# Transposing attention keys inside their load buffers, with one ring of five buffers for every large load

## The chip, the cores and the metric

The kernel runs on one NeuronCore of one Trainium2 chip. The metric is the device time of one execution in microseconds; lower is better. The engines are named as in the profile: PE is TensorE (PEld its weight loads), DVE is VectorE, ACT is ScalarE, POOL is GpSimd and SP is SyncE, whose queue issues nearly all DMAs here.

## The reference

A decode step for two sequences: attention over the last 4096 keys of a cache, beside a dense layer with the mish activation. Both read the same normalised input, and both results are added to it. All data are bfloat16.

```
x: [2, 1, 448]   k_cache, v_cache: [2, 8, 32768, 256]   wq: [448, 4096]   wo: [4096, 448]
w1: [448, 1792]  b1: [1792]   w2: [1792, 448]

xn = (x - mean) / sqrt(var + 1e-5)
q  = xn @ wq                                  # 16 query heads of 256
k, v = the last 4096 positions of the caches  # 8 heads, each for 2 query heads
A  = softmax(q . k / 16) @ v, heads joined, @ wo
h  = xn @ w1 + b1
B  = (h * tanh(softplus(h))) @ w2
out = x + A + B
```

## The kernel before

**Tiles and stages.** The four units `u` = 0 to 3 each hold two key heads of both sequences. The keys of a unit come as two loads k(u,0) and k(u,1), the values as two loads v(u,0) and v(u,1), each 4096 KB: 32 KB in each of 128 partitions. Beside them there are `wq` (3584 KB), `w1` (1568 KB), `w2` (1568 KB in four pieces), a piece `wo(u)` of 896 KB for each unit, and the small `b1` and `x`. SP issues all of them but `x`.

**Buffers.** `ring(name)` takes the next of three 32 KB buffers of `kv_pool`; keys, values, `wq`, `w1` and `w2` all go through it. A load into a buffer waits until what was in it three loads earlier has been read. Two more 32 KB buffers, `kt0` and `kt1` in `kt_pool`, hold transposed keys. `wo` has a pool of its own with two buffers.

**Steps for a unit.** `turns(u, i)` (L266) lets DVE transpose the 32x32 blocks of k(u,i), seen as 4-byte words, in two instructions of 128x4096 from the load buffer into `kt[i]`. After that the load buffer is free. `scores(u, i)` (L340 on) starts a PSUM bank with a mask matmul (L345), adds 32 matmuls over `kt[i]` (L356), lets ACT take the exp (L364), and for i = 1 lets DVE bring the weights into the layout that the values need (L367, and `swap`, L336 to L338). `weigh(u)` adds up the weights (L380, L388). `values(u, g)` (L402) multiplies v(u,g) by the weights, 32 matmuls for a load. `gather(u)`, `finish(u)`, `relay(u)` and `mix_early(u)` (L414 to L482) divide, lay out and multiply by `wo(u)`.

**Beginning.** After constants and the normalisation, PE makes the queries from `wq` (`project`, L291 to L324). `dense_in` (L510, L519) multiplies by `w1` and adds `b1`, and `mish` (L533 to L544) applies the activation. They stand after `turns(0, 1)` in the program.

**End.** The last unit's v(3,1) comes in three pieces (40, 16 and 8 of 64 rows per partition) and `w2` in four, so that PE can begin on each as it lands; `values_fixed` (L435) takes the last two pieces of the values, and `mix` and `dense_out` add into `acc` (L249). `pace(n)` (L575) issues n matmuls whose results nobody reads.

**Order.** The schedule is manual: each engine runs its instructions in the order in which the program writes them, and each load is issued by SP in that order, waiting for its buffer first. The order of loads is wq (two halves), k(0,0), k(0,1), b1, w1, and then for each unit k(u+1,0), v(u,0), k(u+1,1), v(u,1), wo(u), until the last unit's values, wo(3) and `w2`.

Of the kernel before, what the change touches and what calls it, by code (L numbers as in the profile page):

```python
# [11 lines left out]
BF16 = mybir.dt.bfloat16  # L12
FP32 = mybir.dt.float32
# [4 lines left out]
def kernel(  # L18
# [13 lines left out]
    nc = tc.nc  # L32
    P = 128
    G = 4
    J = 4
    R = 4
    RK = 2
# [10 lines left out]
    U = Hkv // KU  # L48
    C = P // J
    CT = W // C  # L50
    T = CT // R
# [16 lines left out]

    lead_pool = ctx.enter_context(tc.tile_pool(name="lead", bufs=1))
    lead_pool.tile([P, 192], BF16, name="lead")  # L70
    kv_pool = ctx.enter_context(tc.tile_pool(name="kv", bufs=3))
    kt_pool = ctx.enter_context(tc.tile_pool(name="kt", bufs=1))
    wo_pool = ctx.enter_context(tc.tile_pool(name="wo", bufs=2))
    p_pool = ctx.enter_context(tc.tile_pool(name="pp", bufs=1))
    consts = ctx.enter_context(tc.tile_pool(name="consts", bufs=1))
# [13 lines left out]
    def ring(name):  # L89
        return kv_pool.tile([P, RK * KE], BF16, tag="kv", name=name)  # L90
# [3 lines left out]
    def load_k(u, r):  # L94
        t = ring("k")
        src = kview[u][:, s0:, :].rearrange("j (c t) d -> c j (t d)", c=C)
        nc.sync.dma_start(out=t[:], in_=src[:, :, r * RK * KE : (r + 1) * RK * KE])
        k_t[u, r] = t
# [19 lines left out]
    nc.scalar.dma_start(out=x_bf[:, :], in_=A_x.flatten_outer_dims())  # L118
    b1_sb = consts.tile([2, F2], BF16)

    wq = ring("wq")
    wq_in = A_wq.flatten().rearrange("(p e) -> p e", p=P)
    half = NS * HW // 2
    for lo in (0, half):
        nc.sync.dma_start(out=wq[:, lo : lo + half], in_=wq_in[:, lo : lo + half])
    wq_t = [wq[:, i * HW : (i + 1) * HW] for i in range(NS)]
    load_k(0, 0)
    load_k(0, 1)
    nc.sync.dma_start(out=b1_sb[:], in_=B_b1.rearrange("(k f) -> k f", k=2))

    ident = consts.tile([P, P], BF16)
    make_identity(nc, ident[:])
# [114 lines left out]
    def add_rows(lhsT, rows, stop=False):  # L247
# [7 lines left out]
                skip_group_check=True,  # L255
            )

    kt = [
        kt_pool.tile([P, T * NB, RK, P // (R * J), J], FP32, name=f"kt{i}") for i in range(NH)
    ]  # L260
    ktm = [
        kt[i][:].bitcast(BF16).rearrange("p (t n) r c (j e) -> p n e t (r c j)", n=NB, e=2)
        for i in range(NH)
    ]

    def turns(u, i):  # L266
        t = k_t.pop((u, i))
        for r in range(RK):
            nc.vector.transpose(  # L269
                out=kt[i][:, :, r, :, :],  # L270
                in_=t[:, r * KE : (r + 1) * KE].bitcast(FP32).rearrange(
                    "p (a c j) -> p a c j", c=P // (R * J), j=J
                ),
            )

    spread = {}
    for n in range(2):
# [9 lines left out]
    def project():  # L287
        q_ps = ps_m.tile([P, 512], FP32, tag="m", name="q_ps")
        for s in range(NS):
            for u in range(U):  # L290
                nc.tensor.matmul(  # L291
                    q_ps[32 * u : 32 * (u + 1), :],
                    lhsT=xs[:, s, :],
                    rhs=wq_t[s][:, u * 512 : (u + 1) * 512],
                    start=(s == 0),
                    stop=(s == NS - 1),
                    skip_group_check=True,
                )
        q_sb = small.tile([P, 4, P], BF16, tag="vs", name="q_sb", bufs=1)
        nc.scalar.copy(out=q_sb[:].rearrange("p a m -> p (a m)"), in_=q_ps[:])  # L300
        qt_ps = ps_m.tile([P, 4, P], BF16, tag="m", name="qt_ps")
        for a in range(4):
            nc.tensor.transpose(qt_ps[:, a, :], q_sb[:, a, :], ident[:])  # L303
        qT = consts.tile([P, 2, U, Bsz, KU, rep], BF16)
        q_v = qt_ps[:].rearrange("p (h c) (u r) -> p c u r h", c=2, u=U)
        for c in range(2):
            for b in range(Bsz):
                nc.vector.tensor_copy(  # L308
                    out=qT[:, c, :, b, :, :], in_=q_v[:, c, :, b : KU * Bsz : Bsz, :]
                )  # L310
        qr_ps = ps_m.tile([P, 2 * NB, U, NQ], FP32, tag="m", name="qr_ps")
        for n in range(NB):
            for e in range(2):
                nc.tensor.matmul(
                    qr_ps[:, 2 * n + e, :, :].rearrange("p u q -> p (u q)"),
                    lhsT=spread[n % 2, e][:].rearrange("p g a -> p (g a)"),
                    rhs=qT[:, n // 2].rearrange("p u b k h -> p (u b k h)"),
                    start=True,
                    stop=True,
                    skip_group_check=True,  # L320
                )
        for g in range(G):
            rows = slice(g * 32, (g + 1) * 32)
            nc.vector.tensor_copy(  # L324
                out=qd[rows, :, :, g, :],
                in_=qr_ps[rows].rearrange("p n u q -> p u n q"),
            )
# [12 lines left out]
    def scores(u, i):  # L340
        if i == 0:
            state["ex"] = small.tile([P, T, 4, NH, J], BF16, tag="ex", name="ex", bufs=1)
        ex = state["ex"]
        sc = ps_sc.tile([P, T, 4, J], FP32, tag="sc", name="sc")
        nc.tensor.matmul(  # L345
            sc[:].rearrange("p t c m -> p (t c m)"),
            lhsT=ident[:],
            rhs=mneg[:].rearrange("p a j -> p (a j)"),
            start=True,
            stop=False,  # L350
            skip_group_check=True,
        )
        for n in range(NB):
            for e in range(2):
                for w in range(4):
                    nc.tensor.matmul(  # L356
                        sc[32 * w : 32 * (w + 1)].rearrange("p t c m -> p t (c m)"),
                        lhsT=qd[:, u, 2 * n + e, :, :].rearrange("p g q -> p (g q)"),
                        rhs=ktm[i][:, n, e, :, 16 * w : 16 * (w + 1)],
                        start=False,  # L360
                        stop=(n == NB - 1 and e == 1),
                        skip_group_check=True,
                    )
        nc.scalar.activation(out=ex[:, :, :, i, :], in_=sc[:], func=ACT.Exp, scale=scale)  # L364
        if i == NH - 1:
            for h in range(NH):
                nc.vector.transpose(  # L367
                    out=p_all[:, :, h * TH : (h + 1) * TH, :].rearrange("p g t q -> p t g q"),
                    in_=ex[:, h * TH : (h + 1) * TH].rearrange(
                        "p t c i m -> p t (c i m)"  # L370
                    ).rearrange("p t (g q) -> p t g q", g=G),
                )
            swap()
# [121 lines left out]

    act_bf = consts.tile([P, NI, 2, Bsz], BF16)

    def load_w1():
        t = ring("w1")
        nc.sync.dma_start(  # L500
            out=t[:, 0 : NS * F2], in_=B_w1.flatten().rearrange("(p e) -> p e", p=P)
        )
        state["w1"] = t

    def dense_in():
        w1 = state.pop("w1")
        w1_v = w1[:, 0 : NS * F2].rearrange("p (s q i) -> p s i q", s=NS, i=NI)
        h_ps = ps_m.tile([P, NI, 2, Bsz], FP32, tag="m", name="h_ps")
        for i in range(NI):
            nc.tensor.matmul(  # L510
                h_ps[:, i, :, :].rearrange("p k b -> p (k b)"),
                lhsT=b1_sb[:, i::NI],
                rhs=halves[:].rearrange("p k b -> p (k b)"),
                start=True,
                stop=False,
                skip_group_check=True,
            )
            for s in range(NS):
                nc.tensor.matmul(  # L519
                    h_ps[:, i, :, :].rearrange("p k b -> p (k b)"),  # L520
                    lhsT=w1_v[:, s, i, :],
                    rhs=xs[:, s, 0 : 2 * Bsz],
                    start=False,
                    stop=(s == NS - 1),
                    skip_group_check=True,
                )
        state["h"] = h_ps
# [37 lines left out]
                act_bf[:, i, k, :], state["w2"][:, at : at + D], stop=(k == 1 and i == NI - 1)  # L565
            )

    load_w1()
    def pace(n, key=None):
        ps = ps_sc.tile([P, T, 4, J], FP32, tag="sc", name="pace")  # L570
        for i in range(n):
# [9 lines left out]
                skip_group_check=True,  # L581
            )

    project()
    turns(0, 0)
    scores(0, 0)
    turns(0, 1)
    dense_in()
    mish()
    scores(0, 1)  # L590
    weigh(0)
    for u in range(U - 1):
        load_k(u + 1, 0)
        load_v(u, 0)
        load_k(u + 1, 1)
        load_v(u, 1)
        load_wo(u)
        turns(u + 1, 0)
        values(u, 0)
        scores(u + 1, 0)  # L600
        turns(u + 1, 1)
        if u == U - 2:
            pace(11, key=ktm[1][:, 0, 0, :, 0:16])
        values(u, 1)
        gather(u)
        finish(u)
        scores(u + 1, 1)
        relay(u)
        mix_early(u)
        if u < U - 2:  # L610
            weigh(u + 1)
    u = U - 1
    load_v(u, 0)
    load_v(u, 1, 0, 40)
    load_wo(u)
    load_v(u, 1, 40, 56)
    load_v(u, 1, 56, TV)
    for part in range(len(w2_parts)):
        load_w2(part)
    pace(3)  # L620
    carry()
    pace(5)
# [57 lines left out]
```

## Time and profile before

| What | Value |
|---|---|
| Median of 3 runs | 188.95 us (188.94 to 189.04) |
| Profiled execution, span from first to last instruction | 187.3 us |
| Time around the span (median less span) | 1.65 us |
| DMA bytes | 77.67 MB from HBM, mean 415 GB/s over the span |
| Busy: PE, DVE, ACT | 84.5 us, 92.8 us, 12.4 us |
| Transposes of the keys (L269) | 16, 70.0 us together, 4414 ns each |

The execution's own total is not printed on the page; the time around its span is therefore taken against the median of the runs. In the profile's groups, "x16 | 70.0, 4414 | 33.8 <-DMA k" means 16 instructions, 70.0 us busy together, 4414 ns each on average, and 33.8 us in which the engine stood idle just before them, most of it until a load of k had landed. In a table by stretches, each engine has its busy time and its count of instructions, and the last three columns are the clock granted to TensorE, the mean busy share of the 16 DMA engines, and GB/s.

### The profile page before, as it was taken

The page shows a single profiled execution, that of the slowest core. Times are in us where ns is not written, and L with a number is a line of the kernel's source. Part 1 is how long each engine was busy: PE and PEld are TensorE (multiplying, and loading weights), DVE is VectorE, ACT ScalarE, POOL GpSimd, SP SyncE. Part 2 cuts the span into 40 slices and gives each one's busy share as a digit, 9 for nine tenths or more (in the row PEclk, how much of TensorE's full clock was granted, in tenths as well). Part 3 has the DMA queues.
Part 4 walks back from the last instruction along what each step waited for, and adds up shares of the span by engine and source line. Part 5 has one row for each costly group of instructions (what it writes and reads, how often), then busy time and mean ns, then how long its engine had stood idle before and what let it go on. Part 6 is the DMA issues. An engine that isn't in the chain of part 4 may idle for free.

```text
span 187.3 us, 1938 instructions
## 1 busy us (share of the span) xinstructions
PE 84.5 (45%) x847; PEld 37.4 (20%) x847; DVE 92.8 (50%) x93; ACT 12.4 (7%) x26; POOL 4.7 (2%) x16
## 2 busy tenths in 40 slices
PE   0373015893119000882047002881065068789694
PEld 0211002551003000340012000430021023424353
DVE  6704397974792097038940296048920593040100
ACT  3003000101000100110001000110001000210100
POOL 8100000000000000000000000000000000000000
PEclk9999999955557955599558855698559756999999
DMA  6999999999999999999999999999999999999991
GB/s 215 422 483 427 441 406 408 454 444 448 427 434 413 416 436 406 462 448 441 441 434 402 413 441 422 445 444 434 448 427 420 420 427 434 434 422 408 416 403 45
DMA packets 4195, 77.78 MB, mean 415 GB/s; under 512 B 470, under 2 KB 732, under 8 KB 1628
## 3 DMA queue, kind: packets, MB, share of 16 engines
q1 hardware_dynamic: 4184, 77.67, 97.1%
q8 instruction: 6, 0.10, 0.2%
q14 instruction: 1, 0.01, 0.0%
q10 hardware_dynamic: 4, 0.00, 0.0%
HBM read 77.67 MB, written 0.00 MB: 415 GB/s over the span
## 4 chain that ended last, share of the span: by engine, by line
DMA 64%; DVE 15%; PE 15%; issue 3%; ACT 1%; SPq 1%
DMA v<-in_A_v_cache_dram 32%; DMA k<-in_A_k_cache_dram 15%; DVE kt L269 12%; DMA w<-in_B_w_dram 11%; DMA wq<-in_A_wq_dram 6%; PE pv L402 4%; PE sc L356 3%; PE h_ps L519 2%; DVE p L367 1%; PE acc L249 1%; PE q_ps L291 1%; PE dn L380 1%; DVE rec L388 1%; PE o L435 1%; ACT ex L364 1%
## 5 line engine op out<-in xcount | busy, mean ns | idle before, releaser
L269 DVE STREAM_TRANSPOSE kt<-k 128x4096 f32<-128x4096 f32 x16 | 70.0, 4414 | 33.8 <-DMA k<-in_A_k_cache_dram 33.8
L402 PE MATMUL pv<-v,p 128*32 128x512 bf16 x244 | 22.5, 534 | 59.5 <-DMA v<-in_A_v_cache_dram 59.5
L356 PE MATMUL sc<-kt,qd 128*32 128x512 bf16 x256 | 19.8, 440 | 13.3 <-DVE kt L269 13.3
L402 PEld LDWEIGHTS <-p 128*32 128x32 bf16 x244 | 8.7, 125 | 72.9 <-issue 49.6
L575 PE MATMUL pace<-mneg,ident 128*128 128x512 bf16 x42 | 12.7, 440 | 0.0
L356 PEld LDWEIGHTS <-qd 128*32 128x32 bf16 x256 | 7.1, 104 | 23.5 <-issue 17.5
L447 DVE TENSOR_TENSOR oT<-o,rec 128x16 bf16<-128x16 f32 x4 | 0.7, 174 | 21.3 <-PE o L420 17.6
L367 DVE STREAM_TRANSPOSE p<-ex 128x512 bf16<-128x512 bf16 x8 | 5.2, 690 | 10.8 <-ACT ex L364 10.8
L364 ACT ACTIVATE ex<-sc 128x512 bf16<-128x512 f32 x8 | 4.8, 597 | 86.7 <-PE sc L356 86.7
L388 DVE TENSOR_REDUCE rec<-dn 128x8 f32<-128x512 f32 x4 | 2.8, 691 | 13.3 <-PE dn L380 13.3
L575 PEld LDWEIGHTS <-ident 128*128 128x128 bf16 x43 | 4.2, 111 | 15.1 <-DVE kt L269 9.2
L414 ACT COPY vs<-pv 128x512 f32<-128x512 f32 x4 | 2.3, 586 | 59.5 <-PE pv L402 59.5
L482 PE MATMUL early<-wo,ox 128*2 128x448 bf16 x24 | 5.0, 352 | 1.9 <-ACT ox L473 1.9
L420 PE MATMUL o<-sel,vs 128*128 128x8 f32 x32 | 4.3, 262 | 2.1 <-ACT vs L414 2.1
L420 PEld LDWEIGHTS o<-sel,vs 128*128 128x128 f32 x32 | 4.2, 196 | 4.5 <-ACT vs L414 4.4
L380 PE MATMUL dn<-p,ones 128*128 128x512 bf16 x8 | 2.8, 440 | 3.8 <-DVE p L338 3.8
L575 PE MATMUL pace<-kt,ident 128*128 128x512 bf16 x1 | 0.6, 607 | 8.7 <-DVE kt L269 8.7
L291 PE MATMUL q_ps<-wq,xs 128*32 128x512 bf16 x28 | 3.8, 624 | 1.4 <-DMA wq<-in_A_wq_dram 1.1
L211 PE MATMUL xr_ps<-ident,xrows 2*128 2x2 bf16 x7 | 1.0, 181 | 7.2 <-DVE xrows L210 7.2
L519 PE MATMUL h_ps<-xs,w 128*128 128x4 bf16 x49 | 3.7, 196 | 0.9 <-DMA w<-in_B_w_dram 0.9
L308 DVE COPY qT<-qt_ps 128x16 bf16<-128x16 bf16 x4 | 0.4, 166 | 6.3 <-PE qt_ps L303 6.3
L345 PE MATMUL sc<-mneg,ident 128*128 128x512 bf16 x8 | 3.5, 434 | 0.0
(71 smaller groups left out, 51.7 us busy)
## 6 DMA issues: line engine op xcount, KB each, us to landing
k<-in_A_k_cache_dram SPq DMA_DIRECT2D x8, 4096.0 KB, 27.7
v<-in_A_v_cache_dram SPq DMA_DIRECT2D x7, 4096.0 KB, 21.2
wq<-in_A_wq_dram SPq DMA_DIRECT2D x2, 1792.0 KB, 8.8
wo<-in_A_wo_dram SPq DMA_DIRECT2D x4, 896.0 KB, 19.0
v<-in_A_v_cache_dram SPq DMA_DIRECT2D x1, 2560.0 KB
w<-in_B_w_dram SPq DMA_DIRECT2D x1, 1568.0 KB, 21.2
v<-in_A_v_cache_dram SPq DMA_DIRECT2D x1, 1024.0 KB, 22.2
w<-in_B_w_dram SPq DMA_DIRECT2D x1, 784.0 KB, 23.5
```

Source lines behind the costliest of these rows:

```text
L269: nc.vector.transpose(out=kt[i][:, :, r, :, :], in_=t[:, r * KE : (r + 1) * KE].bitcast(FP32).rearrange("p (a c j) -> p a c j", c=P // (R ...
L291: nc.tensor.matmul(q_ps[32 * u : 32 * (u + 1), :], lhsT=xs[:, s, :], rhs=wq_t[s][:, u * 512 : (u + 1) * 512], start=(s == 0), stop=(s == N ...
L356: nc.tensor.matmul(sc[32 * w : 32 * (w + 1)].rearrange("p t c m -> p t (c m)"), lhsT=qd[:, u, 2 * n + e, :, :].rearrange("p g q -> p (g q) ...
L364: nc.scalar.activation(out=ex[:, :, :, i, :], in_=sc[:], func=ACT.Exp, scale=scale)
L367: nc.vector.transpose(out=p_all[:, :, h * TH : (h + 1) * TH, :].rearrange("p g t q -> p t g q"), in_=ex[:, h * TH : (h + 1) * TH].rearrang ...
L380: nc.tensor.matmul(dn[:].rearrange("p a q -> p (a q)"), lhsT=ones[:], rhs=p_run[:, i].rearrange("p t q -> p (t q)"), start=(i == 0), stop= ...
L388: nc.vector.tensor_reduce(out=rec[:], in_=dn[:].rearrange("p a q -> p q a"), axis=AXIS.X, op=ALU.add)
L402: nc.tensor.matmul(pv[32 * w : 32 * (w + 1), :, :].rearrange("p x d -> p (x d)"), lhsT=p_run[:, g, 4 * a : 4 * a + 4, :].rearrange("p t q ...
L420: nc.tensor.matmul(po[:, c, :], lhsT=sb[:, x, c::2], rhs=sel[:, x, :], start=(x == 0 and c == 0), stop=(last and x == 1), skip_group_check ...
L482: nc.tensor.matmul(early[:], lhsT=ox[:, i, :], rhs=w[:, i, :], start=False, stop=(u == U - 2 and i == 7),)
L519: nc.tensor.matmul(h_ps[:, i, :, :].rearrange("p k b -> p (k b)"), lhsT=w1_v[:, s, i, :], rhs=xs[:, s, 0 : 2 * Bsz], start=False, stop=(s ...
L575: nc.tensor.matmul(ps[:].rearrange("p t c m -> p (t c m)"), lhsT=ident[:], rhs=rhs, start=True, stop=True, skip_group_check=True,)
```

## The change

Three things are changed together.

1. `turns` writes the transposed blocks back over the key load's own buffer. `kt0` and `kt1` are gone, and `scores` reads the load buffer through a new view, `turned(u, i)`. The buffer stays taken until the scores have been computed.
2. The ring has five buffers instead of three; the memory is that of the two `kt` buffers. The issues of loads are spread through the program so that each stands after the step that frees its buffer.
3. `w1` is the first load, `b1` the second, and `wq` comes as one load instead of two halves. `dense_in` and `mish` stand ahead of `project`.

```diff
-    kv_pool = ctx.enter_context(tc.tile_pool(name="kv", bufs=3))
-    kt_pool = ctx.enter_context(tc.tile_pool(name="kt", bufs=1))
+    kv_pool = ctx.enter_context(tc.tile_pool(name="kv", bufs=5))
...
+    w1 = ring("w1")
+    nc.sync.dma_start(
+        out=w1[:, 0 : NS * F2], in_=B_w1.flatten().rearrange("(p e) -> p e", p=P)
+    )
+    nc.sync.dma_start(out=b1_sb[:], in_=B_b1.rearrange("(k f) -> k f", k=2))
     wq = ring("wq")
-    wq_in = A_wq.flatten().rearrange("(p e) -> p e", p=P)
-    half = NS * HW // 2
-    for lo in (0, half):
-        nc.sync.dma_start(out=wq[:, lo : lo + half], in_=wq_in[:, lo : lo + half])
+    nc.sync.dma_start(
+        out=wq[:, 0 : NS * HW], in_=A_wq.flatten().rearrange("(p e) -> p e", p=P)
+    )
...
     load_k(0, 0)
     load_k(0, 1)
-    nc.sync.dma_start(out=b1_sb[:], in_=B_b1.rearrange("(k f) -> k f", k=2))
+    load_k(1, 0)
...
     def turns(u, i):
-        t = k_t.pop((u, i))
+        t = k_t[u, i]
         for r in range(RK):
-            nc.vector.transpose(
-                out=kt[i][:, :, r, :, :],
-                in_=t[:, r * KE : (r + 1) * KE].bitcast(FP32).rearrange(
-                    "p (a c j) -> p a c j", c=P // (R * J), j=J
-                ),
-            )
+            blocks = t[:, r * KE : (r + 1) * KE].bitcast(FP32).rearrange(
+                "p (a c j) -> p a c j", c=P // (R * J), j=J
+            )
+            nc.vector.transpose(out=blocks, in_=blocks)
+
+    def turned(u, i):
+        return k_t[u, i][:].rearrange(
+            "p (r t n g e) -> p n e r t g", r=RK, t=T, n=NB, g=P // R, e=2
+        )
...
-                        rhs=ktm[i][:, n, e, :, 16 * w : 16 * (w + 1)],
+                        rhs=kt[:, n, e, w // 2, :, 16 * (w % 2) : 16 * (w % 2 + 1)],
...
+    dense_in()
+    mish()
+    load_v(0, 0)
     project()
+    load_k(1, 1)
     turns(0, 0)
     scores(0, 0)
+    load_v(0, 1)
+    load_wo(0)
     turns(0, 1)
-    dense_in()
-    mish()
     scores(0, 1)
+    load_k(2, 0)
     weigh(0)
     for u in range(U - 1):
-        load_k(u + 1, 0)
-        load_v(u, 0)
-        load_k(u + 1, 1)
-        load_v(u, 1)
-        load_wo(u)
         turns(u + 1, 0)
         values(u, 0)
         scores(u + 1, 0)
+        if u < U - 2:
+            load_v(u + 1, 0)
+            load_k(u + 2, 1)
+        else:
+            load_v(u + 1, 1, 0, 40)
+            load_wo(u + 1)
+            load_v(u + 1, 1, 40, 56)
+            load_v(u + 1, 1, 56, TV)
+            for part in range(len(w2_parts)):
+                load_w2(part)
         turns(u + 1, 1)
         if u == U - 2:
-            pace(11, key=ktm[1][:, 0, 0, :, 0:16])
+            pace(11, key=turned(u + 1, 1)[:, 0, 0, 0, :, 0:16])
         values(u, 1)
         gather(u)
         finish(u)
         scores(u + 1, 1)
+        if u < U - 2:
+            load_v(u + 1, 1)
+            load_wo(u + 1)
+            if u < U - 3:
+                load_k(u + 3, 0)
+            else:
+                load_v(u + 2, 0)
...
     u = U - 1
-    load_v(u, 0)
-    load_v(u, 1, 0, 40)
-    load_wo(u)
-    load_v(u, 1, 40, 56)
-    load_v(u, 1, 56, TV)
-    for part in range(len(w2_parts)):
-        load_w2(part)
     pace(3)
```

More of the change, by code (lines that the diff above doesn't have):

```diff
@@ L256, in add_rows @@
             )
[L258 to L264, printed above, removed]
     def turns(u, i):
-        t = k_t.pop((u, i))
+        t = k_t[u, i]
         for r in range(RK):
-            nc.vector.transpose(
-                out=kt[i][:, :, r, :, :],
-                in_=t[:, r * KE : (r + 1) * KE].bitcast(FP32).rearrange(
-                    "p (a c j) -> p a c j", c=P // (R * J), j=J
-                ),
-            )
+            blocks = t[:, r * KE : (r + 1) * KE].bitcast(FP32).rearrange(
+                "p (a c j) -> p a c j", c=P // (R * J), j=J
+            )
+            nc.vector.transpose(out=blocks, in_=blocks)
[3 more added lines that the diff above has]
+        )
     spread = {}
@@ L343, in scores @@
         ex = state["ex"]
+        kt = turned(u, i)
         sc = ps_sc.tile([P, T, 4, J], FP32, tag="sc", name="sc")
@@ L496 @@
     act_bf = consts.tile([P, NI, 2, Bsz], BF16)
[L498 to L501, printed above, removed]
-        )
-        state["w1"] = t
     def dense_in():
-        w1 = state.pop("w1")
         w1_v = w1[:, 0 : NS * F2].rearrange("p (s q i) -> p s i q", s=NS, i=NI)
@@ L566, in dense_out @@
             )
-    load_w1()
     def pace(n, key=None):
```

## The prediction

> **What bounds the kernel now.** I read the busy slices and the DMA queues first, then the chain that ended last, then the busy time by stretches, and last the waits of the load queue, because the change is about loads and buffers.
>
> ```profile
> PE 84.5 (45%) x847; PEld 37.4 (20%) x847; DVE 92.8 (50%) x93; ACT 12.4 (7%) x26; POOL 4.7 (2%) x16
> ...
> DMA  6999999999999999999999999999999999999991
> ...
> q1 hardware_dynamic: 4184, 77.67, 97.1%
> q8 instruction: 6, 0.10, 0.2%
> ...
> DMA 64%; DVE 15%; PE 15%; issue 3%; ACT 1%; SPq 1%
> ```
> No engine is busy for more than half of the span. The 16 DMA engines are busy for 97.1% of it with the kernel's own 77.67 MB; the chain gives them only 64%, since it jumps to whatever released a step.
>
> ```profile
> 4.00:20.00 16.00, 6.64 (x49) 2.55 (x50) 6.30 (x33) 1.87 (x2) 1.33 (x6) 1.00 1.04 444
> 20.00:40.00 20.00, 9.31 (x91) 5.49 (x91) 17.48 (x5) 0.79 (x2) 0.00 (x0) 0.95 0.99 425
> ...
> 100.00:120.00 20.00, 5.52 (x65) 2.07 (x64) 8.77 (x2) 0.79 (x2) 0.00 (x0) 0.66 1.01 433
> ...
> 160.00:180.00 20.00, 16.54 (x167) 7.86 (x167) 3.24 (x8) 1.92 (x5) 0.00 (x0) 1.00 0.98 412
> ```
> The last two columns are DMA share and GB/s. The share is 1 in every stretch (a packet counts where it starts, so it may pass 1). GB/s divided by share is 427, 429, 429 and 420: time per byte hardly depends on the stage. The nine stretches from 4 to 180 us average 431 GB/s.
>
> ```profile
> SPq L105 <- DVE kt L269: 55.7, 6, 11.5
> ```
> ```profile
> 30.38 0.55 SPq L97 DMA_DIRECT2D k<-in_A_k_cache_dram  x1
> ```
> ```profile
> 13.84 21.16 DMA w<-in_B_w_dram
> ```
> The load queue waits long for buffers (the waits' line), which looks like starvation. It is not: the load with the shortest lead, k(1,0), is issued at 30.38 (the timeline's line), while w1, ahead of it, lands only at 13.84+21.16 = 35.00 (the chain's piece). Even there 4.6 us of work is queued, and the stretch 20 to 40 shows no hole.
>
> **The change part by part.** Bytes: the same tensors once each, 77.67 MB. I walked the queue in both orders. Before: wq (two halves), k(0,0), k(0,1), b1, w1, k(1,0), and then v(0,0), k(1,1), v(0,1), wo(0), k(2,0) and so on. After: w1, b1, wq, k(0,0), k(0,1), k(1,0), and from there the identical list to the end. The sum of bytes up to each load from k(1,0) on is unchanged, so with full engines each lands when it does now.
>
> w1 first: 1568 KB is 1.606 MB, at 431 GB/s 3.7 us. So wq, k(0,0) and k(0,1) land 3.7 us later: wq at 11.9+3.7 = 15.6, k(0,0) at 21.6+3.7 = 25.3, k(0,1) at 35.0. dense_in (PE 35.04 to 39.2, some 4.2 us) and mish (1.2 us on DVE) move ahead of project, into time in which PE waits for wq: xs is there at 8.9, so they take PE to about 13.5. project's 28 matmuls (3.8 us) and its chain to qd (13.84 to 17.88, 4.0 us) then end at 23.4; the first scores need a transposed half at 25.3+4.4 = 29.7. The cover is 6 us; without it only the u = 0 scores move, and they have the leads below. ACT's 1.28 us table load for the exp moves along; project's copy (L300) queues behind it, inside the same cover. On SP the first five big loads wait for nothing; the sixth, v(0,0), now waits for dense_in to read w1, with 30 us of loads ahead of it. Cost 0.
>
> wq as one DMA: in the trace's packet records a 14,336-byte packet takes 0.535 us and a 32,768-byte one 1.213, or 26.8 and 27.0 bytes per ns. Each engine moves eight 28,672-byte rows instead of sixteen halves: 8 x (1.070 - 1.062) = 0.06 us off every engine. The Trainium skill (DMA: Bandwidth & Descriptors, "Anatomy of one DMA") puts some 2 us fixed on each DMA of the GpSimd path, against bytes at 436 GB/s; were that paid in the stream, one DMA fewer would make 186.9, but 16 full engines leave no room for it.
>
> Ring of five: a K buffer is now held until its scores are read, not only until it is transposed. I ask of each load when its buffer is free and when the load ahead lands. k(2,0) needs scores(0,1): 35.0 + 8.8 of transposes + 4 = 48; ahead is wo(0) at about 77. v(1,0) needs scores(1,0), now ending by 63; ahead is k(2,0) at about 87. v(1,1) needs scores(1,1), 82.4 now; ahead is k(2,1), about 106. v(3,1) needs scores(3,0), near 144; ahead is v(3,0), 168.7. The shortest lead becomes about 24 us instead of 4.6. Leads are not time: nothing was idle before, so the gain is 0, and SP's longer waits delay nobody.
>
> In-place transposes: 16 as before. The nearest row is the same instruction into another tile:
>
> ```profile
> L269 DVE STREAM_TRANSPOSE kt<-k 128x4096 f32<-128x4096 f32 x16 | 70.0, 4414 | 33.8 <-DMA k<-in_A_k_cache_dram 33.8
> ```
> 4,096 elements in 4.41 us, about one each ns. No row shows it in place; small copies inside p (L337) and from p into px (L336) both take 0.30, so I take 4.41, with twice that as the upper bound; a shorter one gains nothing, as DVE waits for the loads. The scores read 128x512 with another step; the bounds are what 32 of them take now at full clock (1.92 us, from 161.04) and at half clock (4.12 us, from 39.59), so 0 to 2.2 us more. Only the last, scores(3,1), could show. Its cover:
>
> ```profile
> 168.74 1.91 PE L402 MATMUL pv<-v,p 128*32 128x512 bf16 x32 [0.77 <-DMA v<-in_A_v_cache_dram]
> ...
> 174.92 1.26 PE L402 MATMUL pv<-v,p 128*32 128x512 bf16 x20 [1.79 <-DMA v<-in_A_v_cache_dram]
> ...
> 179.56 0.96 PE L435 MATMUL o<-p,v 128*128 128x8 bf16 x32 [0.27 <-DMA v<-in_A_v_cache_dram]
> ```
> Brackets are PE's idle time before each: 0.77+1.79+0.27 = 2.8 us can be lost before the end moves. I take 0 since only the step changes, not the shape; either end is covered.
>
> The tail: PE's order differs only in where dense_in's 112 rows stand, so every filler matmul (pace) and split load at the end stays.
>
> Sum: 0.06 us off the stream, the rest 0. Span 187.3 - 0.1 = 187.2. The runs shown have 188.94 to 189.04, median 188.95, so 1.65 us lie around the span; the forecast is 188.9. From no change a measurement here can tell about 0.2%, 0.38 us.
>
> **The rivals.** *A: the uneven end moves.* The DMA engines don't finish together:
>
> ```profile
> 182.50:183.00 0.50, 0.50 (x14) 0.46 (x12) 0.00 (x0) 0.00 (x0) 0.00 (x0) 1.00 0.58 222
> 183.00:183.50 0.50, 0.50 (x16) 0.45 (x14) 0.00 (x0) 0.00 (x0) 0.00 (x0) 1.00 0.40 154
> 183.50:184.00 0.50, 0.50 (x16) 0.43 (x12) 0.00 (x0) 0.00 (x0) 0.00 (x0) 1.00 0.31 111
> 184.00:185.00 1.00, 0.87 (x14) 0.41 (x8) 0.08 (x1) 0.04 (x1) 0.00 (x0) 1.00 0.02 8
> ```
> The work left at 182.5 is 0.58x0.5+0.40x0.5+0.31x0.5+0.02 = 0.67 us of all 16; spread evenly it would end at 183.2 instead of about 184.4. The q8 row gives one cause: six program blocks take 0.2% x 16 x 187.3 / 6, about 1.0 us each, of one engine. Six of 16 engines then end late. Evenly spread: 188.9 - 1.2 = 187.7. Two blocks on one engine: 189.9. Against both: the instruction count and all loads per engine stay. Chance beyond 0.2%: 0.09 down, 0.08 up. The Trainium skill (Runtime: NRT & Kernel Launch, "Instruction fetch mechanics") calls the cost of a 16 KiB block mostly hidden; by that this rival is worth 0, while the uneven shares speak for a place in the stream.
>
> *B: deeper queues raise the rate.* At 444 GB/s, the figure of 4 to 20 us, where several loads are queued, the 75.8 MB of 4 to 180 us would take 170.7 us and the kernel 183.6. Against it: share and rate rise together, 444/1.04 = 427. Chance 0.05.
>
> *C, slower: the in-place transpose takes longer, and DVE becomes the bound.* DVE goes in order: four transposes of t for each u, then about 7 us until the next u's may start (scores 4, exp 0.6, p 2.2). Starting at 25.3, the last transpose ends at 25.3+16t+3x7 if DVE never waits for loads; scores(3,1) now start at 161.0, with 2.8 us to lose. So it decides from t = 7.3. At twice (8.8): 187.1 - 163.8 = 23 us, 212. For it: reading and writing the same rows might serialise. Against: in the one-per-ns row the engine already reads and writes the same memory. Chance 0.05.
>
> *D: the ring gives less than it says*, and a load waits for a buffer until the queue is dry. By the leads some step must be over 24 us late first; beyond that each us costs a us, a whole load 9.7 (198.6). Chance 0.02.
>
> **How the numbers follow.** Forecast within 0.2%: 0.71. Faster 0.09 (A) + 0.05 (B) = 0.14; slower 0.08 (A) + 0.05 (C) + 0.02 (D) = 0.15. The range takes in most of A on both sides and leaves out B, C and D (0.12) and A's far ends: 188.2 to 189.6.
>
> **What would show it.** Right: q1 still 77.67 MB, share 1 and some 431 GB/s in all stretches, k(3,1) landing near 147.2 and the first v(3,1) part near 174.9; transposes of about 4.4 us; SP waiting longer for buffers; dense_in at 9 to 13.5. Wrong: a stretch below 0.95 before 180 us, transposes over 7 us, PE waiting on the transposes rather than on v in the last 20 us, or DMA shares that drop all at once, or later, after 182.5.

## The result, and the profile after

The changed kernel takes 189.54 us (median of 14 runs, 189.23 to 189.70), the kernel before 188.94 on the same chip. The ratio is 1.0028, 95% interval 1.0020 to 1.0036: slower by 0.6 us, more than the 0.2% that a measurement here can tell. The profiled execution took 189.60 us with a span of 187.8 us, 0.5 more than the span before.

Nearly everything the prediction said of the parts can be read off the page. These are its rows for the engines, the busy slices, the queues, the chain and the transposes:

```profile
PE 89.5 (48%) x847; PEld 39.7 (21%) x847; DVE 92.9 (49%) x93; ACT 12.4 (7%) x26; POOL 4.7 (2%) x16
...
DMA  6999999999999999999999999999999999999991
...
q1 hardware_dynamic: 4040, 77.67, 96.8%
q8 instruction: 6, 0.10, 0.2%
...
DMA 82%; PE 11%; DVE 3%; issue 1%; SPq 1%; POOL 0%; ACT 0%; POOLq 0%; DVEq 0%
...
L267 DVE STREAM_TRANSPOSE k<-k 128x4096 f32<-128x4096 f32 x16 | 70.0, 4414 | 24.9 <-DMA k<-in_A_k_cache_dram 24.9
```

The bytes are the same, the DMA engines are full from the second slice to the last but one, and the in-place transpose takes 4414 ns, to the nanosecond what the other one took. The stretches say the same (last two columns: DMA share and GB/s):

```profile
4.00:20.00 16.00, 9.06 (x94) 5.88 (x95) 5.26 (x29) 1.90 (x3) 1.31 (x6) 1.00 1.03 444
20.00:40.00 20.00, 6.01 (x46) 2.11 (x45) 14.74 (x11) 0.60 (x1) 0.00 (x0) 1.00 0.99 428
...
100.00:120.00 20.00, 5.91 (x65) 2.39 (x64) 8.77 (x2) 0.63 (x2) 0.00 (x0) 0.67 1.00 431
...
160.00:180.00 20.00, 16.28 (x154) 7.64 (x154) 3.23 (x8) 1.92 (x5) 0.00 (x0) 1.00 0.99 415
```

The first row has 9.06 us of PE where it had 6.64: dense_in now runs there (9.0 to 13.3). The longer leads are there too. From the timeline of the load queue:

```profile
59.11 0.54 SPq L104 DMA_DIRECT2D v<-in_A_v_cache_dram  x1
```

This is v(1,0), issued at 59.11, while k(2,0), the load ahead of it, lands at 86.5: a lead of some 27 us.

The two spans differ by 0.5 us, the medians by 0.6. The page before does not print its execution's own time; with the 1.8 us that lie around the span after (189.60 - 187.8) it would be about 189.1, an estimate, a little over the median of its kernel.

So where is the half microsecond? The timeline of the consumers shows a delay at the first transposes and again near the end (start, length, and in brackets the idle time before). The first fence is of the changed kernel, the second has two rows of the kernel before that the prediction does not show:

```profile
25.65 8.77 DVE L267 STREAM_TRANSPOSE k<-k 128x4096 f32<-128x4096 f32 x2 [2.45 <-DMA k<-in_A_k_cache_dram]
147.50 8.77 DVE L267 STREAM_TRANSPOSE k<-k 128x4096 f32<-128x4096 f32 x2 [10.35 <-DMA k<-in_A_k_cache_dram]
169.02 1.91 PE L401 MATMUL pv<-v,p 128*32 128x512 bf16 x32 [0.97 <-DMA v<-in_A_v_cache_dram]
175.20 1.26 PE L401 MATMUL pv<-v,p 128*32 128x512 bf16 x20 [1.79 <-DMA v<-in_A_v_cache_dram]
179.90 0.96 PE L434 MATMUL o<-p,v 128*128 128x8 bf16 x32 [0.32 <-DMA v<-in_A_v_cache_dram]
185.29 0.38 DVE L646 CAST res<-acc 2x224 bf16<-2x224 f32 x1 [2.77 <-PE acc L252]
```
```profile
147.23 8.77 DVE L269 STREAM_TRANSPOSE kt<-k 128x4096 f32<-128x4096 f32 x2 [10.39 <-DMA k<-in_A_k_cache_dram]
...
184.92 0.38 DVE L646 CAST res<-acc 2x224 bf16<-2x224 f32 x1 [2.75 <-PE acc L249]
```

The first transposes start at 25.65 where the prediction's walk through the queue gave 25.3. The three rows of values begin at 169.02, 175.20 and 179.90 instead of 168.74, 174.92 and 179.56: 0.28, 0.28 and 0.34 late. The transposes at 147.50 began at 147.23 before, 0.27 earlier, and the last copy at 184.92, 0.37 earlier.

A load has landed when the slowest of the 16 DMA engines has finished its part. The trace has the 16 landings of each load. For k(0,0) the earliest is at 24.52 and the latest at 25.62, 0.03 before the transposes start: a spread of 1.10 us; before it was 0.68 (20.88 to 21.55). The last piece of `w2` lands between 182.53 and 184.96, before between 182.64 and 184.59. Its mean over the engines moved only from 183.47 to 183.59, the latest by 0.37.

The delay is not simply carried from the first load to the last. From k(1,0) to v(1,0), 45 to 96 us, the latest landing of each load is 0.07 to 0.09 us earlier than before (k(1,1) 65.09 against 65.17); from k(2,1) on (106.61 against 106.43) it is 0.17 to 0.42 later. Which engine comes last changes on the way, and the rest of the text has to explain that too.

The stretches at the end show the same thing as a longer, thinner tail:

```profile
182.50:183.00 0.50, 0.50 (x10) 0.29 (x10) 0.02 (x1) 0.01 (x1) 0.00 (x0) 1.00 0.57 221
183.00:183.50 0.50, 0.50 (x16) 0.45 (x12) 0.00 (x0) 0.00 (x0) 0.00 (x0) 1.00 0.43 170
183.50:184.00 0.50, 0.50 (x16) 0.45 (x12) 0.00 (x0) 0.00 (x0) 0.00 (x0) 1.00 0.34 126
184.00:185.00 1.00, 0.97 (x19) 0.62 (x15) 0.00 (x0) 0.00 (x0) 0.00 (x0) 1.00 0.13 47
```

The first stretch is as busy as before (0.57 against 0.58); the last still has 0.13 where 0.02 was left. In all kernels below whose own time is known beside the trace, the execution ends 4.5 to 4.7 us after the latest landing (here 189.60 - 184.96 = 4.64). So the question for the experiments: which part of the change makes some engines late at the start?

### The profile page after: what moved, and what is told of

Same layout as the page of the kernel before. It is cut to its first block, busy times and chain, and to the rows that moved or that the text cites. A ratio compares the mean times of both kernels' runs of the same rounds, so it can differ in the third digit from the quotient of the medians.

```text
span 187.8 us, 1939 instructions
## 1 busy us (share of the span) xinstructions
PE 89.5 (48%) x847; PEld 39.7 (21%) x847; DVE 92.9 (49%) x93; ACT 12.4 (7%) x26; POOL 4.7 (2%) x16
## 3 DMA queue, kind: packets, MB, share of 16 engines
q1 hardware_dynamic: 4040, 77.67, 96.8%
HBM read 77.67 MB, written 0.00 MB: 414 GB/s over the span
## 4 chain that ended last, share of the span: by engine, by line
DMA 82%; PE 11%; DVE 3%; issue 1%; SPq 1%; POOL 0%; ACT 0%; POOLq 0%; DVEq 0%
DMA v<-in_A_v_cache_dram 82%; PE pv L401 6%; PE h_ps L510 2%; PE acc L252 1%; DVE halves L141 1%; PE o L434 1%; PE pace L565 1%; DVE sel L201 1%; PE h_ps L501 1%; PE xr_ps L214 1%; DVE xs L222 0%; SPq L110 0%; SPq L104 0%; DVE mneg L190 0%; DVE xn_bf L167 0%
## 5 line engine op out<-in xcount | busy, mean ns | idle before, releaser
L267 DVE STREAM_TRANSPOSE k<-k 128x4096 f32<-128x4096 f32 x16 | 70.0, 4414 | 24.9 <-DMA k<-in_A_k_cache_dram 24.9
L401 PE MATMUL pv<-v,p 128*32 128x512 bf16 x244 | 23.0, 542 | 48.1 <-DMA v<-in_A_v_cache_dram 48.1
L355 PE MATMUL sc<-k,qd 128*32 128x512 bf16 x256 | 23.2, 491 | 20.0 <-DVE k L267 20.0
L355 PEld LDWEIGHTS <-qd 128*32 128x32 bf16 x256 | 8.7, 111 | 31.5 <-issue 28.8
L565 PE MATMUL pace<-mneg,ident 128*128 128x512 bf16 x42 | 11.7, 412 | 0.0
L481 PE MATMUL early<-wo,ox 128*2 128x448 bf16 x24 | 6.5, 426 | 1.9 <-ACT ox L472 1.9
L419 PE MATMUL o<-sel,vs 128*128 128x8 f32 x32 | 5.1, 286 | 2.1 <-ACT vs L413 2.1
L419 PEld LDWEIGHTS o<-sel,vs 128*128 128x128 f32 x32 | 4.9, 228 | 4.5 <-ACT vs L413 4.4
L565 PE MATMUL pace<-k,ident 128*128 128x512 bf16 x1 | 0.6, 607 | 8.4 <-DVE k L267 8.4
L289 PE MATMUL q_ps<-wq,xs 128*32 128x512 bf16 x28 | 3.2, 630 | 2.7 <-DMA wq<-in_A_wq_dram 2.7
```

Of the source, the lines that this page charges most:

```text
L267: nc.vector.transpose(out=blocks, in_=blocks)
L289: nc.tensor.matmul(q_ps[32 * u : 32 * (u + 1), :], lhsT=xs[:, s, :], rhs=wq_t[s][:, u * 512 : (u + 1) * 512], start=(s == 0), stop=(s == N ...
L355: nc.tensor.matmul(sc[32 * w : 32 * (w + 1)].rearrange("p t c m -> p t (c m)"), lhsT=qd[:, u, 2 * n + e, :, :].rearrange("p g q -> p (g q) ...
L401: nc.tensor.matmul(pv[32 * w : 32 * (w + 1), :, :].rearrange("p x d -> p (x d)"), lhsT=p_run[:, g, 4 * a : 4 * a + 4, :].rearrange("p t q ...
L419: nc.tensor.matmul(po[:, c, :], lhsT=sb[:, x, c::2], rhs=sel[:, x, :], start=(x == 0 and c == 0), stop=(last and x == 1), skip_group_check ...
L481: nc.tensor.matmul(early[:], lhsT=ox[:, i, :], rhs=w[:, i, :], start=False, stop=(u == U - 2 and i == 7),)
```

## Experiments

Each kernel is given by its edit against the changed kernel, unless said otherwise. Times are medians; the ratio is to the kernel before on the same chip, whose median was 188.84 to 188.98 in every group. The ratio is not the quotient of the two medians and can differ from it by 0.1 to 0.2%.

### The ring alone, the start alone

**e1: the five-buffer ring and the transposes in place, with the old beginning.**

```diff
-    w1, b1, wq (whole), k(0,0), k(0,1), k(1,0)      # first loads
+    wq (two halves), k(0,0), k(0,1), b1, w1, k(1,0)
...
-    dense_in()
-    mish()
-    load_v(0, 0)
     project()
+    load_v(0, 0)
     turns(0, 0)
     scores(0, 0)
     ...
     turns(0, 1)
+    dense_in()
+    mish()
     scores(0, 1)
```

> The ring of five and the in-place transposes alone; the first loads (wq in two halves, k(0,0), k(0,1), b1, w1) and the place of dense_in are those of the kernel before. Start theory (the first transfer leaves the slowest of the 16 DMA engines some 0.4 us later, and that lag stays to the end): 188.95 us, ratio 1.000, the first transposes start at 21.6 us. Ring theory (deeper queues or transposing in place cost the time): 189.5 us, ratio 1.003. Block theory (a program block, fetched earlier because dense_in stands earlier, meets another DMA engine): 188.95.

Measured: 188.95, ratio 0.9996 (0.9972 to 1.0019); the kernel before had 188.97. The ring, the in-place transposes and the other step of the score reads cost nothing together that can be seen. The loss is in the beginning.

**e2: the new beginning on the kernel before** (three buffers, `kt0` and `kt1`, old issue places; the diff is against that kernel).

```diff
+    load w1, b1, wq (whole), k(0,0)        # was: wq (halves), k(0,0), k(0,1), b1, w1
...
+    dense_in()
+    mish()
+    load_k(0, 1)
     project()
     turns(0, 0)
     scores(0, 0)
     turns(0, 1)
-    dense_in()
-    mish()
     scores(0, 1)
```

> The new start alone (w1, b1, wq as one load first; dense_in and mish ahead of project), with three buffers and separate transposed keys as in the kernel before. Start theory: 189.5 us, ratio 1.003, last 16 DMA engines as uneven as in the changed kernel. Ring theory: 188.95. Block theory: 189.5.

Measured: 190.73 (189.84 to 192.13), ratio 1.0113 (1.0087 to 1.0140): 1.8 us, some three times the loss of the whole change. The profiled execution is the fastest of the six, so the trace shows the smaller part of that. With three buffers the new order does run the queue dry. The first fence has a row of the waits of the load queue in e2, the second two rows of its busy times by stretch.

```profile
SPq L105 <- DVE kt L271: 72.6, 7, 16.4
```
```profile
60.00:80.00 20.00, 6.56 (x64) 2.40 (x63) 10.48 (x3) 1.18 (x2) 0.00 (x0) 0.57 0.99 416
...
62.00:66.00 4.00, 2.51 (x30) 0.85 (x23) 1.33 (x1) 0.60 (x1) 0.00 (x0) 0.59 0.92 340
```

The wait for a transpose is 72.6 us (55.7 before), and from 62 to 66 the engines are at 0.92 of busy and 340 GB/s: v(0,1) is issued at 61.74 and k(1,1), the load ahead, lands at 63.67 on the mean of its engines (63.15 to 64.65), about 2 us of lead. The mean landing of v(0,1) is 0.6 us later than in the changed kernel. The packet records show that it is not the gap alone: most of the first 32 KB packets after it take 1.3 to 2.1 us, where 1.21 is usual. So e2 adds a fault of its own and does not measure the beginning by itself. It does show that the new order needs the ring.

### Which piece of the beginning

**e3: `b1` after `wq`. e4: `wq`, still one load, ahead of `w1` and `b1`.** `dense_in` stays early in both.

```diff
     w1                      # e3
-    b1
     wq (whole)
+    b1
...
+    wq (whole)              # e4
     w1
     b1
-    wq (whole)
```

> The changed kernel with b1 issued behind wq instead of between w1 and wq, so that the small load no longer stands second. If the two-row load behind the first big one is what staggers the start: 188.95 us. If w1's place as the first load does it: 189.5, as the changed kernel. Ring theory and block theory: 189.5.

> The changed kernel with wq (still one load of 28 KB rows) issued first, then w1 and b1; dense_in still runs ahead of project. Start theory, with w1's rows of 12,544 bytes as the bad first load: 188.95 us, because wq is first. Start theory, with the single undivided wq as the culprit: 189.5 or more. Block theory: 189.5, since dense_in stands where the changed kernel has it. Ring theory: 189.5.

Measured: e3 189.50, ratio 1.0033 (1.0021 to 1.0045); e4 189.37, ratio 1.0036 (1.0011 to 1.0061). The place of the small `b1` does not matter, and putting `wq` first as one load helps little here (0.40 us over the kernel before; three of the 12 runs of e4 took 190.7 to 191.1, for which no run gives a reason). Either `wq` has to come in halves, or the early `dense_in` costs.

**e5: `wq` in halves ahead of `w1` and `b1`. e7: `w1` first, `wq` in halves. e9: e1 with `wq` in one load. e6: `w1` first in two loads of half rows, `wq` in halves.**

```diff
+    wq (half), wq (half)    # e5
     w1
     b1
-    wq (whole)
...
     w1, b1                  # e7
-    wq (whole)
+    wq (half), wq (half)
...
-    w1, b1                  # e6
-    wq (whole)
+    w1 (half), w1 (half), b1
+    wq (half), wq (half)
```

> The changed kernel with wq in two halves (14 KB rows) as the first load, then w1 and b1; dense_in still ahead of project. First-load theory (the rows of the very first load decide how unevenly the 16 DMA engines start): 188.95 us, ratio 1.000. Undivided-wq theory (28 KB rows in the start cost it): 188.95. Block theory (dense_in's early place moves the program blocks): 189.4, ratio 1.0025.

> The changed kernel with wq in two halves again; w1 stays first and dense_in early. First-load theory: 189.5 us, as the changed kernel. Undivided-wq theory: 188.95. Block theory: 189.5.

> Ring of five and in-place transposes with the old start, but wq as one load of 28 KB rows at the head; dense_in at its old late place. First-load theory: 189.35 us, as with wq undivided at the head and dense_in early. Undivided-wq theory: 189.35. Block theory: 188.95.

> The changed kernel with w1, still first, in two loads of 6 KB rows, and wq in two halves behind it. First-load theory: smaller first rows let the engines start more evenly, so 188.95 us or a little under. Undivided-wq theory: 188.95. Block theory: 189.5.

Measured: e5 188.95, ratio 0.9996 (0.9981 to 1.0011). The early `dense_in` and `mish`, `w1` ahead of the keys and the ring all stay, and the loss is gone. e7: 189.16, 1.0000 (0.9978 to 1.0022); e9: 189.11, 1.0007 (0.9999 to 1.0016); e6: 189.21, 1.0022 (1.0008 to 1.0035). These three are too near each other to separate "`w1` first" from "`wq` in one piece", and e7 against e3 and e4 compares two chips.

**f1 to f4: the square, on one chip.** f1 is the changed kernel once more, f2 the kernel of e7, f3 that of e4, f4 that of e5; their edits are above.

> The changed kernel once more, beside the next three on one chip, as one corner of a square of four: which load is first (w1 or wq) by how wq is loaded (whole or in halves); dense_in stands early in all four. If the two parts of the start add up: 189.5 us here. If chips explain the difference between the earlier calls: near 189.2.

> Corner w1 first, wq in halves. Adding parts: 189.15 us (w1 first costs 0.2). If the chip explained the earlier figure: the same as the changed kernel beside it.

> Corner wq first, wq whole. Adding parts: 189.3 us (the whole wq costs 0.35). If only w1's first place matters: 188.95.

> Corner wq first, wq in halves: the start of the kernel before with dense_in early, a ring of five and transposes in place. Adding parts, and every form of the start theory: 188.95 us, as the kernel before. If the ring or the transposes in place cost anything on this chip: above 189.1.

| first load | `wq` in one load | `wq` in halves |
|---|---|---|
| `w1` | f1: 189.46, 1.0032 (1.0019 to 1.0045) | f2: 189.50, 1.0031 (1.0019 to 1.0043) |
| `wq` | f3: 189.23, 1.0022 (1.0013 to 1.0031) | f4: 188.97, 0.9998 (0.9985 to 1.0011) |

With `w1` first the form of `wq` makes no difference; with `wq` first its halves are worth 0.26 us. What counts is the very first load. By the medians, 0.5 to 0.7 us are lost if it is `w1` (0.2 on the chip of e7 and e6); 0.4 if it is the whole of `wq` (e4, f3; 0.13 in e9); 0 to 0.13 if it is half of `wq` (e1, e5, f4).

**g4: half of `wq` first, then `w1` and `b1`. g3: `wq` in four quarters. g6: `wq` first, its first load with rows of 12,544 bytes, the row of `w1`.**

```diff
+    wq (first half)         # g4
     w1
     b1
-    wq (whole)
+    wq (second half)
...
+    wq (quarter) x4         # g3
     w1
     b1
-    wq (whole)
...
+    wq[:, 0:6272], wq[:, 6272:14336]      # g6
     w1
     b1
-    wq (whole)
```

> The changed kernel mended as little as possible: one half of wq goes first, w1 and b1 second, the other half of wq third; everything else as changed, dense_in still ahead of project. First-load theory: 188.95 us. If w1's early place as such costs the time, first or second: 189.3 or more.

> The kernel with wq first, in four loads of 7 KB rows instead of two of 14 KB, to see whether still smaller first rows start the engines more evenly and beat both kernels. First-load theory by row size alone: 188.8 to 188.95 us. If it is w1's place in memory and not its row size that makes a bad first load: 188.95, as with halves.

> wq first, cut at 6272 columns instead of in the middle, so that the first load has rows of 12,544 bytes like w1's, but lies in wq (28,672 bytes from row to row). If the row size makes the bad first load: 189.4 us. If it is where w1 lies and how its rows follow each other: 188.95.

Measured: g4 188.92, ratio 0.9999 (0.9990 to 1.0007); g3 189.11, 1.0007 (0.9998 to 1.0016); g6 189.02, 0.9995 (0.9984 to 1.0006). g4 is the change with one load moved ahead of it, and the loss is gone. g6 says that it is not the row size of `w1`, nor the size of the load, which is the same. Smaller first rows of `w1` did not help (e6 189.21, e7 189.16 on the same chip). In g3 the engines start most evenly of all (k(0,0) spread over 0.45 us), and it is not faster: a more even start than that of g4 (0.65) bought nothing.

The stretches from 1.5 to 3.5 us show the start, first of the changed kernel, then of g4. A packet's time counts where it starts, so 2.26 or 0.21 are possible.

```profile
1.50:2.00 0.50, 0.00 (x0) 0.00 (x0) 0.50 (x2) 0.50 (x1) 0.50 (x1) 1.00 1.63 254
2.00:2.50 0.50, 0.00 (x0) 0.00 (x0) 0.50 (x3) 0.50 (x1) 0.50 (x3) 1.00 0.50 100
2.50:3.00 0.50, 0.00 (x0) 0.00 (x0) 0.50 (x3) 0.07 (x1) 0.50 (x1) 1.00 0.69 226
```
```profile
1.50:2.00 0.50, 0.00 (x0) 0.00 (x0) 0.50 (x2) 0.50 (x1) 0.50 (x1) 1.00 2.26 405
2.00:2.50 0.50, 0.00 (x0) 0.00 (x0) 0.50 (x3) 0.50 (x1) 0.50 (x3) 1.00 0.21 57
2.50:3.00 0.50, 0.00 (x0) 0.00 (x0) 0.50 (x3) 0.07 (x1) 0.50 (x1) 1.00 0.37 143
```

In g4 14 of the 16 engines start their first packet before 2.0 us (405 GB/s of packets begun), as 15 did before (434); with `w1` first only ten do (254, of smaller packets), and the rest follow up to 1 us later. The end of g4 answers:

```profile
182.50:183.00 0.50, 0.50 (x16) 0.46 (x12) 0.00 (x0) 0.00 (x0) 0.00 (x0) 1.00 0.48 186
183.00:183.50 0.50, 0.50 (x16) 0.46 (x12) 0.00 (x0) 0.00 (x0) 0.00 (x0) 1.00 0.40 149
183.50:184.00 0.50, 0.50 (x16) 0.46 (x12) 0.00 (x0) 0.00 (x0) 0.00 (x0) 1.00 0.25 86
184.00:185.00 1.00, 0.65 (x12) 0.34 (x8) 0.32 (x1) 0.28 (x1) 0.00 (x0) 1.00 0.00 0
```

No load's packet starts after 184.0, and the latest landing is at 184.35 instead of 184.96: the whole 0.6 us. Its first transposes, with k(0,0) spread over 0.65 us, start where the prediction put them, at 25.3 to within a tenth:

```profile
25.21 8.77 DVE L268 STREAM_TRANSPOSE k<-k 128x4096 f32<-128x4096 f32 x2 [1.22 <-DMA k<-in_A_k_cache_dram]
```

### A lag put in by hand

These three start from f4, the kernel without a loss, and add loads of 0.26 MB that nobody reads, right after `b1`, into the free part of the `w1` buffer. In g1 and g5 they are two loads of 8 rows of 16 KB, in g2 one load over all 128 partitions.

```diff
+    w1[8*i : 8*i+8, free : free+8192]       <- k_cache[0, i, 0:256]    # g1, i = 0, 1
+    w1[32*i : 32*i+32 : 4, free : free+8192] <- k_cache[0, i, 0:256]   # g5, i = 0, 1
+    w1[:, free : free+1024]                 <- k_cache[0, 0, 0:512]    # g2
```

> The kernel with wq in halves first (188.95 us) plus 256 KB that nobody reads, in two loads of eight 16 KB rows right behind b1, so that they lie on 8 of the 16 DMA engines: 2 x 0.607 us more for each of those eight, nothing for the others. If the slowest engine sets the end and a lag is never made up: up to +1.2 us, 190.15 (less if none of the eight is among those that fetch program blocks). If the end goes by bytes, the mean of the engines: +0.6, 189.55. If the engines make up a lag while the queue is deep: 188.95 to 189.55.

> The same 256 KB as one load of 128 rows of 2 KB at the same place, spread over all 16 engines: 8 x 0.08 = 0.64 us for each. Slowest-engine theory and byte theory both: +0.6, 189.55 to 189.6. The difference to the kernel with the lag on half of the engines is what tells them apart.

> The lag on half of the engines once more, with the same 256 KB in two loads of eight 16 KB rows, but the rows go to every fourth partition (0 to 28, and 32 to 60) instead of 16 neighbouring ones, since in the first try those loads took 1.4 to 1.9 us a packet and held up all engines. Slowest-engine theory: 190.15 us (+1.2; less if few of the eight engines fetch program blocks), with the earliest landing of each later load where it was and the latest 1.2 us later. Byte theory: 189.55.

**g1** does not test the lag: 192.45, ratio 1.0183 (1.0166 to 1.0199). The rows into neighbouring partitions held up the whole stream, as its stretches show:

```profile
14.00:15.00 1.00, 0.00 (x0) 0.00 (x0) 0.00 (x0) 0.00 (x0) 0.00 (x0) 1.00 1.91 561
15.00:16.00 1.00, 0.00 (x0) 0.00 (x0) 0.00 (x0) 0.00 (x0) 0.00 (x0) 1.00 1.46 215
16.00:17.00 1.00, 0.10 (x1) 0.10 (x1) 0.00 (x0) 0.00 (x0) 0.00 (x0) 1.00 0.44 66
```

Twelve of its 16 KB packets took 1.4 to 1.9 us instead of 0.61, the 32 KB packets beside them up to 3.6 instead of 1.21, and every engine came out late: by 2.9 to 3.6 us at k(0,0) and 2.6 to 3.8 at the end, compared with f4.

**g2**: 189.61, ratio 1.0035 (1.0022 to 1.0047). All engines are late alike: the earliest landing at the end is 183.19 instead of 182.61 in f4, the latest 184.95 instead of 184.37, both by 0.58; 0.26 MB at 431 GB/s is 0.61.

**g5** has the bytes of g1, but in every fourth partition, and runs clean: 189.39, ratio 1.0030 (1.0016 to 1.0045). In its profile k(0,0) is spread over 1.74 us (0.93 in f4), and at the end the earliest engine is where it was (182.58) and the latest at 185.25, 0.88 later than in f4. Two rows of the end of g5 by stretches:

```profile
183.00:183.50 0.50, 0.50 (x13) 0.46 (x14) 0.00 (x0) 0.00 (x0) 0.00 (x0) 1.00 0.76 292
...
184.00:185.00 1.00, 0.99 (x23) 0.72 (x17) 0.00 (x0) 0.00 (x0) 0.00 (x0) 1.00 0.14 50
```

A lag put on some engines at 15 us is still there 170 us later: no engine takes over another's bytes. But the 12 runs of g5 fall into two groups, eight at 189.21 to 189.47 and four at 189.97 to 190.34, and the profile, at 189.97, is of one of the four. The time is therefore no proof of the slowest-engine reckoning: its 190.15 fits the four, while the median, 189.39, lies even under the 189.55 of the reckoning by bytes. The likely reason, not shown by these runs, is that a lag costs its whole size only if the engine that has it also ends last.

## Why the prediction failed

**What held.** The same 77.67 MB at share 1 and some 431 GB/s in every stretch; transposes of 4.4 us; `dense_in` at 9.0 to 13.3; leads of some 27 us and more for the keys and values; nothing for the score reads (e1). SP's waits did not grow as was said: 153 us in all against 152, the output's left out. Rivals B (a higher rate), C (a slower transpose) and D (a dry queue) did not happen, though e2 shows D is real with three buffers. The time around the span, taken as 1.65 us, is 1.8 in the profiled executions (189.60 - 187.8; e1 188.99 - 187.2); that is no part of the difference. The gain of 0.06 us from one load of `wq` cannot be seen, and one load more costs nothing near 2 us either (f1 189.46, f2 189.50); as the first load, the undivided `wq` is the slower form (f3 against f4).

**The step that failed** is "w1 first", and in it "Cost 0", which rests on the sentence ahead of it: "The sum of bytes up to each load from k(1,0) on is unchanged, so with full engines each lands when it does now." The sum of bytes gives the mean over the engines, and the mean did land there: k(1,0) at 44.46 against 44.41 before, and k(0,0) at 24.99 in the changed kernel, 24.94 in g4, 24.97 in f4. What waits for a load, and in the end the kernel, waits for the slowest engine. The walk moved the start of the stream to another load and took the engines' stagger, the differences between their starts, as given. At k(0,0) that stagger measured 1.10 us instead of 0.68, 0.42 more, and the last landing of all came 0.37 later, most of the 0.5 us between the spans. The trace before showed that there is such a stagger. In its first stretches the engines start unequally and their first packets are slow; no term of the sum was made from that:

```profile
1.50:2.00 0.50, 0.00 (x0) 0.00 (x0) 0.50 (x2) 0.50 (x1) 0.50 (x1) 1.00 2.36 434
2.00:2.50 0.50, 0.00 (x0) 0.00 (x0) 0.50 (x3) 0.50 (x1) 0.50 (x3) 1.00 0.16 29
2.50:3.00 0.50, 0.00 (x0) 0.00 (x0) 0.50 (x3) 0.08 (x1) 0.50 (x1) 1.00 0.42 143
3.00:3.50 0.50, 0.00 (x0) 0.00 (x0) 0.43 (x5) 0.00 (x0) 0.44 (x2) 1.00 0.82 344
```

It did not show that another first load would change the stagger; only the runs did. One of the prediction's own signs of being wrong is on the page: after 182.5 the DMA shares drop later, with 0.13 left from 184 to 185 instead of 0.02. That 189.54 lies within the stated range is luck as far as the sum goes: the room above came from rival A, not from a term.

**Rival A** had the place, the uneven end, and gave a move upward 0.08, but had the wrong reason for it. It let only the six program blocks decide who ends late. They do make late engines: at the end of the changed kernel ten engines land from 182.53 to 183.50 and six from 184.19 to 184.96, and a block fetched at 29.37 lifts the spread from 1.10 at k(0,0) to 1.90 at k(0,1). The Trainium skill (Runtime: NRT & Kernel Launch, "Instruction fetch mechanics") calls the cost of crossing into a new 16 KiB block mostly hidden; in this full stream it is not hidden for the DMA engine that fetches the block, as the 0.80 us more of spread show. Yet the change did not move that: there are six blocks before and after. What it moved is the lag that the first load leaves, on which the blocks come on top. That would explain why the delay is not to be seen from 45 to 96 us: until a late starter fetches a block, another engine comes last. In the changed kernel the delay returns with the loads behind the block fetched at 99.92, and in the repeat, f1, it shows clearly only from v(3,0) on (168.95 against 168.70), behind the block fetched at 163.46. The trace does not name the engine of a packet, so this stays an inference.

**How far this is shown.** That the first load decides is shown by f1 to f4 and g4; that a lag put on engines lasts, by the landings of g5; that the latest engine sets the end, by 4.5 to 4.7 us in every profile. The link from the start's stagger to the end is looser. Leaving out e2 and the kernels with added loads, and measuring the spread at the last early load that no block has touched (for f1 `wq`, else `wq` or k(0,0)): six kernels have 0.95 us or more, and five of them take 189.29 to 189.60 in the profiled execution. The sixth, e5, has 1.24 and takes 188.95; one engine alone is late there, and by the landings it seems to have fetched no block. Nine have less than 0.95; eight take 188.88 to 189.08, and f3 189.23. The line at 0.95 was drawn afterwards and is a fine one: g6 with 0.94 takes 189.02, e3 with 0.95 189.33. One profile of each does not give more. **Why `w1` is a bad first load stays open.** It is not its row size (g6), not `b1` behind it (e3), not what uses it early (g4). The loss was 0.5 to 0.7 us in e3, f1 and f2 and 0.2 on the chip of e7; whether the chip or the place of the tensor in memory has a part was not tried. One pattern was not tried by itself either: the first loads that lose clearly, `w1` and the whole of `wq`, are read from memory in one unbroken run, the pieces of `wq` with gaps between their rows. But e6, half rows of `w1` with gaps, was 0.2 us slower too.

No version beats both kernels. g4, f4 and e1 equal the kernel before, and keep the longer leads without a use for them.

## What to carry to other kernels

In a kernel that the DMA stream fills from end to end, count each load as landed when its slowest engine is done, and look at the spread of the 16 landings in the first loads as well as in the last: here a lag made in the first 3 us was paid at the end. Moving which load comes first is then not always free, even if bytes, order and leads are unchanged further on. Where leads do not limit the rate, as here, more buffers brought nothing; they only made an order possible that starved with fewer (e2).

## What the runs showed of the hardware

- The first packets of nearly all engines are slow and unequal. With half of `wq` first (14,336-byte packets) the first packets of nearly all engines start from 1.75 to 2.3 us and take 0.9 to 1.7 us, later ones 0.535. With `w1` first (12,544 bytes, 0.469 us later on) four to six of the engines start only from 2.1 to 2.9, and two or three packets take 1.6 to 2.05 (the changed kernel, f1 and f2; in e7, where the loss was only 0.2 us, 1.5 at most).
- Sixteen rows of 16 KB into 16 neighbouring partitions made most of their packets take 1.4 to 1.9 us and left every engine 2.6 to 3.8 us late at the end (g1); into every fourth partition the same packets took 0.61 each, and the mean landing at the end moved by 0.5 us, about what their bytes take (g5).
- A transpose of 32x32 blocks in place takes exactly as long as one into another tile, 4414 ns for 128x4096 four-byte words.
